# Where the scores of a pair's last 64 queries stand in an attention round (causal attention, then a PReLU MLP)

## The chip, the cores and the metric

The kernel runs on one core of a Trainium2 chip. The metric is the device time of one execution in microseconds (us). Before the change it is 618.56 us, the median of three runs (618.24 to 618.84). The profiled execution took 617.75 us; its span, from the first to the last instruction, is 616.0 us, so 1.75 us lie outside the span. Durations below come from that one execution.

## The reference

```python
scores = scale * np.matmul(q, k.transpose(0, 1, 3, 2))   # 4 batches, 12 heads, 448 queries, head size 64
scores = np.where(mask, -1000000000.0, scores)           # causal
attn = softmax(scores)                                   # max, exp, sum + 1e-9, division
x = np.matmul(attn, v) reshaped to (1792, 768)
h = x @ w_in                                             # w_in 768 x 2048
g = np.maximum(h, 0) + alpha * np.minimum(h, 0)
out = g @ w_out                                          # w_out 2048 x 768
```

All inputs are float64 in memory (the weights are taken apart into float32 parts on the chip) and the output is float32.

## The kernel before

**The two stages.** The attention takes the first 150 us of the span, the MLP the rest; some steps of the MLP's preparation are mixed into the attention: the weight pieces of `start_piece` go through ScalarE (Abs, line 250), GpSimd (clamp, line 253), four VectorE steps (lines 256, 260, 263 and 264) and a GpSimd addition (line 267).

**A pair.** The attention works on 24 pairs of heads. A pair has two heads j = 0, 1 and 448 queries in three blocks: 128 (i = 0), 128 (i = 1), 128 (i = 2), and a last block of 64 queries that both heads share (i = 3): their 64 queries each are laid side by side into one operand `qd` of 128 columns, loaded apart from the other queries (line 362). `scores(p, 0)` (S0) makes the scores of i = 1 and 0 for both heads and `scores(p, 1)` (S1) those of i = 2; both use 64 rows of the array per head (line 424), twelve matmul passes in all. `scores(p, 2)` (S2) makes the scores of the last queries, two passes of 128 rows (line 416). VectorE then masks and takes the maximum (MXij, line 436), ScalarE takes the exponential with its row sum (EXij, line 451), VectorE turns the sums into reciprocals (RC, lines 460 and 461), GpSimd multiplies (NOij, line 405), TensorE transposes (PTi, line 480, 16 passes), ScalarE and VectorE copy the transposes out of PSUM (Cij, lines 401 and 403: C10, C20 and C30 on ScalarE, C00 and C21 on VectorE), and TensorE multiplies with V (AV, line 499). XF, XN, XH and XL then write the result's parts for the MLP; XL (line 561) is the last reader of AV's bank.

**The round.** `attention()` runs rounds n = 0 to 27. The text `ORDER` lists the steps of a round by name with a lag: `S0+1` means S0 of pair n - 1. Each engine takes its instructions in the order of that text. `ROUNDS` has texts of their own for rounds 2 and 3, and round 26 is `ORDER` with one step moved. Before the change a round's order on each engine is, with the lag behind the plus sign:

- TensorE: AV+4, S2+2, PT1+3, PT0+3, PT2+3, PT3+3, S0+1, S1+1 (and SF+1, which is S2 for pairs 0 and 23 only)
- VectorE: MX11+2, MX20+2, MX21+2, MX00+2, MX01+2, XF or XN+4, MX30+2, EG, XL+4, C00+3, C21+3, RC+2, ED, MX10+1. EG and ED are the VectorE steps of the weight pieces; E2, at the head of the round, holds four of them in round 25
- ScalarE: EX10+2, EX11+2, EX20+2, EX00+2, EX21+2, EX01+2, XH+4, C10+3, EX30+2, C20+3, C30+3, EA
- GpSimd: NO00+3, NO10+3, NO21+3, NO11+3, NO20+3, NO30+3, weight work, NO01+2

Round 4 is the first with all steps; its AV is that of pair 0, at 16.08 us. Pair 23 has its S0, S1 and S2 in round 24.

**Banks.** Eight PSUM banks serve S (five per pair), PT (five) and AV (one). A bank goes to the next step in the program that asks for one, in about the order in which the last reader of each stands in the program, and the new owner's first matmul waits for that reader. S0 and S1 take two banks each, one per head.

**Loads.** SyncE issues the loads in program order: `LK` and `LQ` of pair n stand at the head of round n; `LQ` loads the two halves of `qr` and then the two pieces of `qd`.

Of the kernel before, what the change touches and what calls it, by code (L numbers as in the profile page):

```python
# [34 lines left out]
LOADV = {0: 3, 1: 2, 2: 2, 9: 4, 10: 3, 12: 2, 13: 3, 14: 2}  # L35
TURNS = [(0, 0), (0, 1), (0, 2), (0, 5), (1, 0), (1, 1), (1, 3), (1, 4), (0, 3), (0, 4), (1, 2), (1, 5)]
ORDER = """
E2+4 LK+0 LQ+0 LT+4 NO00+3p NO10+3p MX11+2 NO21+3p NO11+3p EX10+2 EX11+2 MX20+2 NO20+3p MX21+2 EX20+2 NO30+3p MX00+2 EX00+2 AV+4 S2+2 LV+4 PT1+3 PT0+3 PT2+3 EX21+2 MX01+2 EX01+2 XF+4 XN+4 XH+4 C10+3a MX30+2 EG+4 XL+4 EX30+2 EH+4 C00+3d C21+3d RC+2 ED+4 NO01+2p C20+3a PT3+3 S0+1 S1+1 SF+1 C30+3a EA+4 MX10+1 ST+4
"""
ROUNDS = {2: """  # L40
LK+0 LQ+0 MX11+2 EX10+2 EX11+2 MX00+2 EX00+2 MX01+2 EX01+2 MX20+2 EX20+2 MX21+2 EX21+2 RA+2 NO10+2p NO11+2p NO00+2p NO01+2p MX30+2 S0+1 S1+1 PT1+2 PT0+2 MX10+1 MX11+1 EX30+2 RB+2 NO20+2p NO21+2d NO30+2p
""", 3: """
LK+0 LQ+0 EX10+2 EX11+2 MX00+2 EX00+2 MX01+2 EX01+2 MX20+2 S2+2 EX20+2 MX21+2 PT2+3 EX21+2 C10+3a C00+3d MX30+2 EX30+2 C21+3d RC+2 NO01+2p C20+3a PT3+3 S0+1 S1+1 SF+1 C30+3a MX10+1
"""}
FIRST = """
0: gh.0Y gh.0X gl.0Y gl.0X abs.i0.1 clamp.i0.1 cast.o0.0 cast.o1.0 st
# [77 lines left out]
def kernel(  # L124
# [19 lines left out]
    NQ = S // QP  # L144
    LQ = S - NQ * QP
# [25 lines left out]
    def bank(name):  # L171
        return banks["a"].tile([P, 512], F32, tag="a", name=name)
# [176 lines left out]
    def half(j):  # L349
        return slice(j * D, (j + 1) * D)  # L350
# [59 lines left out]
    def scores(p, n):  # L410

        if n == 2:
            ps = bank(f"s_{p}_{n}")[:, :S]
            nc.tensor.matmul(ps, qd[p % 3], T["k", p], start=True, stop=True)  # L416
            T["s", p, NQ, 0] = ps
            return
        banks = [bank(f"s_{p}_{n}_{j}") for j in range(2)]
        o = 0  # L420
        for i in ((1, 0), (2,))[n]:
            lim = (i + 1) * QP
            for j, ps in enumerate(banks):
                nc.tensor.matmul(  # L424
                    ps[:, o : o + lim], T["q", p][half(j), i * QP : (i + 1) * QP],
                    T["k", p][half(j), :lim], start=(o == 0), stop=(n > 0 or i == 0),
                )
                T["s", p, i, j] = ps[:, o : o + lim]
            o += lim
# [26 lines left out]
    def row_rec(p, cols=slice(0, 2 * NQ + 1)):  # L456
        sm = T["sm", p]
        if ("r", p) not in T:
            T["r", p] = ap["b2"].tile([P, 2 * NQ + 1], F32, tag="rs", name=f"rs_{p}")
        nc.vector.tensor_tensor(out=sm[:, cols], in0=sm[:, cols], in1=least[:, cols], op=ALU.add)  # L460
        nc.vector.reciprocal(T["r", p][:, cols], sm[:, cols])
# [55 lines left out]
    def flush(to):  # L517
        while to:
            to.pop(0)()
# [62 lines left out]
    def run(it, n=None):  # L582
# [3 lines left out]
    steps = {  # L586
        "LV": load_v_next, "RC": row_rec, "RA": lambda p: row_rec(p, slice(0, 4)), "RB": lambda p: row_rec(p, slice(4, 2 * NQ + 1)), "AV": av, "XH": x_hi, "XN": x_hi_plain, "XF": x_sums, "XL": x_lo, "ST": lambda p: flush(stores),
    }
# [17 lines left out]
            add(steps, f"EX{i}{j}", row_exp, i, j)  # L606
            add(choice, f"NO{i}{j}", row_norm, i, j)
    edge = (0, len(pairs) - 1)
    steps["SF"] = lambda p: p in edge and scores(p, NQ - 1)
    steps["S2"] = lambda p: p in edge or scores(p, NQ - 1)  # L610
    steps["ED"] = lambda p: [fn() for fn in plan.pop(p + 4, ())]
    steps["EH"] = lambda p: [fn() for fn in mid.pop(p + 4, ())]
    steps["EG"] = lambda p: [fn() for fn in gap.pop(p + 4, ())]
# [4 lines left out]
    def order_of(text):  # L618
        order = []
        for w in text.split():  # L620
            name, lag = w.split("+")
            if name in choice:
                eng = {"a": nc.scalar, "d": nc.vector, "p": nc.gpsimd}[lag[-1]]
                order.append((int(lag[:-1]), name, lambda p, fn=choice[name], eng=eng: fn(p, eng)))
            else:
                order.append((int(lag), name, steps[name]))
        return order

    def attention(hooks):
        order, first = order_of(ORDER), {n: order_of(x) for n, x in ROUNDS.items()}  # L630
        first[26] = order_of(ORDER.replace("C10+3a ", "").replace("EH+4 ", "EH+4 C10+3a "))
        last = max(lag for lag, *_ in order)
        for n in range(len(pairs) + last):
            for lag, name, fn in first.get(n, order):
                if 0 <= n - lag < len(pairs):
                    fn(n - lag)
                    for hook in hooks.get((n - lag, name), ()):
                        hook()
# [282 lines left out]
    def after(p, name, fn, *args):  # L921
        hooks.setdefault((p, name), []).append(lambda: fn(*args))
# [4 lines left out]
    with tc.manual_schedule():  # L927
# [33 lines left out]
        last = len(pairs) - 1  # L961
# [5 lines left out]
        after(6, "LQ", load_next)  # L967
        after(3, "LV", lambda: nc.sync.dma_start(out=alpha_sb, in_=alpha.rearrange("(c p) -> p c", p=P)))
        after(20, "LV", lambda: ts(out=less, in0=alpha_sb[:, :GC], scalar1=-1.0, scalar2=None, op0=ALU.mult))
        after(last, "SF", scores_done)  # L970
        after(last - 1, "C30", h_plain, 0, 4)
        after(last - 1, "AV", h_plain, 4, 10)
        after(last, "C21", h_act, 0, "Y")
# [128 lines left out]
```

## Time and profile before

| What | Value |
|---|---|
| median of 3 runs | 618.56 us (618.24 to 618.84) |
| the profiled execution | 617.75 us, span 616.0 us |
| PE busy | 607.5 us (99%) |
| VectorE (DVE), ScalarE (ACT), GpSimd (POOL) busy | 498.5, 285.2, 391.2 us |
| granted TensorE clock, mean | 0.999 of full speed |
| chain that ended last | PE 91%, DVE 3%, DMA 2%, ACT 1%, issue 1%, POOL 1% |

PE is TensorE's matmuls, PEld its weight loads, SP is SyncE's queue. A matmul's end is modelled, so PE busy is no measure of its idle time inside a stage: the distance from one step's start to the next step's start is.

### The profile page before, as it was taken

To read this page: it belongs to the slowest core of one execution; us is meant where nothing else is said; L and a number is where in the kernel's file an instruction comes from. 1 tells how busy PE (TensorE), PEld (TensorE's weight loads), DVE (VectorE), ACT (ScalarE), POOL (GpSimd) and SP (SyncE) were. 2 spreads that over 40 slices of the span, in tenths; PEclk is the share of its full clock that TensorE was granted. 3 is DMA by queue.
4 is the path that set the end of the run, shared out by engine and by line. 5 is a ranking of instruction groups with operands and counts; after the bars stand their busy time and mean duration, and the time that the engine had idled before them with its cause. 6 is when DMAs were issued, how large, how long until landed. Compare 5 with 4: busy or idle time off the path is not lost.

```text
span 616.0 us, 10906 instructions
## 1 busy us (share of the span) xinstructions
PE 607.5 (99%) x3527; PEld 530.5 (86%) x3527; DVE 498.5 (81%) x1120; ACT 285.2 (46%) x782; POOL 391.2 (64%) x525
## 2 busy tenths in 40 slices
PE   8999999999999999999999999999999999999997
PEld 4666666667879999999999999999999999999997
DVE  5899999999777787898798789868987887895364
ACT  6989888896657643333232323232332323231110
POOL 6666587867475669756875686486668756862120
PEclk9999999999999999999999999999999999999999
DMA  7765477634884578657757756676576577554725
GB/s 171 197 191 164 131 216 215 191 123 130 271 294 153 182 248 276 197 170 226 216 160 231 224 167 204 209 229 198 171 228 217 156 231 225 165 174 140 245 89 193
DMA packets 88298, 120.40 MB, mean 195 GB/s; under 512 B 12273, under 2 KB 66257, under 8 KB 88241
## 3 DMA queue, kind: packets, MB, share of 16 engines
q1 hardware_dynamic: 87584, 118.36, 62.7%
q0 software_dynamic: 336, 0.89, 0.6%
q8 instruction: 28, 0.46, 0.3%
q10 hardware_dynamic: 320, 0.46, 0.2%
q14 instruction: 30, 0.24, 0.1%
HBM read 105.00 MB, written 14.68 MB: 194 GB/s over the span
## 4 chain that ended last, share of the span: by engine, by line
PE 91%; DVE 3%; DMA 2%; ACT 1%; issue 1%; POOL 1%; POOLq 0%; ACTq 0%; SPq 0%; DVEq 0%
PE o L789 35%; PE heldY L691 11%; PE heldX L691 8%; PE a L499 7%; PE pt L480 6%; PE heldZ L691 6%; PE s L424 5%; PE s L416 3%; PE h_V L691 3%; PE heldW L691 3%; PE h_Y L691 1%; PE h_W L691 1%; PE h_X L691 1%; PE h_Z L691 1%; DMA lo_T<-low_T 1%; ACT p L451 1%
## 5 line engine op out<-in xcount | busy, mean ns | idle before, releaser
L797 DVE TENSOR_TENSOR acc<-o,acc 128x384 f32<-128x384 f32 x196 | 107.4, 551 | 76.3 <-PE o L789 75.6
L405 POOL TENSOR_SCALAR p<-p,rs 128x128 f32<-128x128 f32 (+3 forms) x165 | 82.2, 520 | 42.2 <-ACT ptf L401 27.1
L451 ACT ACTIVATE p<-s,nm 128x256 f32<-128x256 f32 (+3 forms) x168 | 82.0, 497 | 14.8 <-DVE nm L436 13.2
L436 DVE CUSTOM_DVE_ANT_0 s<-s,mask 128x128 f32<-128x128 f32 (+3 forms) x168 | 71.2, 480 | 9.0 <-PE s L424 5.3
L789 PE MATMUL o<-wo,g_X 128*128 128x384 f32 x336 | 77.8, 339 | 0.5 <-DVE g_X L755 0.5
L789 PE MATMUL o<-wo,g_Z 128*128 128x384 f32 x336 | 77.5, 338 | 0.0
L789 PE MATMUL o<-wo,g_W 128*128 128x384 f32 x336 | 77.3, 337 | 0.3 <-POOL g_W L755 0.3
L789 PE MATMUL o<-wo,g_Y 128*128 128x384 f32 x336 | 76.9, 336 | 0.0
L789 PEld LDWEIGHTS o<-wo,g_X 128*128 128x128 f32 x336 | 60.7, 188 | 4.0 <-DVE g_X L755 0.8
L789 PEld LDWEIGHTS o<-wo,g_Z 128*128 128x128 f32 x336 | 60.7, 188 | 3.1
L789 PEld LDWEIGHTS o<-wo,g_W 128*128 128x128 f32 x336 | 60.6, 188 | 0.6 <-POOL g_W L755 0.6
L789 PEld LDWEIGHTS o<-wo,g_Y 128*128 128x128 f32 x336 | 60.6, 188 | 0.0
L480 PEld LDWEIGHTS pt<-ident,p 128*128 128x128 f32 x384 | 43.3, 140 | 12.5 <-issue 7.9
L499 PEld LDWEIGHTS a<-ptf,v 128*64 128x64 f32 x384 | 25.4, 136 | 31.0 <-issue 12.1
L267 POOL TENSOR_TENSOR y_i<-y_i,x_i 128x384 f32<-128x384 f32 x32 | 33.0, 1030 | 29.6 <-DVE x_i L264 29.6
L267 POOL TENSOR_TENSOR y_o<-y_o,x_o 128x384 f32<-128x384 f32 x32 | 33.4, 1042 | 25.4 <-DVE x_o L264 25.4
L480 PE MATMUL pt<-ident,p 128*128 128x128 f32 x384 | 47.3, 274 | 1.2 <-POOL p L405 0.8
L499 PE MATMUL a<-ptf,v 128*64 128x448 f32 (+3 forms) x384 | 46.8, 386 | 0.1
L424 PE MATMUL s<-kr,qr 64*128 64x384 f32 (+2 forms) x288 | 39.5, 395 | 0.7 <-DMA kr<-in_k_dram 0.5
L401 ACT ACTIVATE ptf<-pt 128x512 f32<-128x512 f32 (+1 forms) x72 | 38.1, 573 | 3.0 <-PE pt L480 2.9
L755 POOL TENSOR_TENSOR g_Z<-t_Z,g_Z 128x384 fp32r<-128x384 f32 (+1 forms) x15 | 18.5, 1231 | 31.4 <-ACT g_Z L750 31.4
L250 ACT ACTIVATE x_i<-raw_i 128x384 f32<-128x384 f32 x32 | 17.8, 556 | 42.6 <-DMA raw_i<-in_moe_w_in_dram 42.6
(189 smaller groups left out, 1340.2 us busy)
## 6 DMA issues: line engine op xcount, KB each, us to landing
lo_T<-low_T SPq DMA_DIRECT2D x28, 512.0 KB, 4.7
lo_B<-low_B SPq DMA_DIRECT2D x25, 512.0 KB, 5.0
raw_i<-in_moe_w_in_dram SPq DMA_DIRECT2D x32, 384.0 KB, 3.6
raw_o<-in_moe_w_out_dram SPq DMA_DIRECT2D x32, 384.0 KB, 3.6
lo_T<-low_T SPq DMA_DIRECT2D x28, 384.0 KB, 3.6
lo_B<-low_B SPq DMA_DIRECT2D x25, 384.0 KB, 4.0
lo_N<-low_N SPq DMA_DIRECT2D x16, 512.0 KB, 4.7
lo_N<-low_N SPq DMA_DIRECT2D x16, 384.0 KB, 4.5
```

The source lines that it names most:

```text
L267: nc.gpsimd.tensor_tensor(out=y, in0=y, in1=xf, op=ALU.add)
L401: eng.activation(out, x, AF.Copy, scale=side)
L405: eng.tensor_scalar(out=out, in0=x, scalar1=side, scalar2=1.0, op0=ALU.mult, op1=ALU.mult)
L424: nc.tensor.matmul(ps[:, o : o + lim], T["q", p][half(j), i * QP : (i + 1) * QP], T["k", p][half(j), :lim], start=(o == 0), stop=(n > 0 or ...
L436: nc.vector.tensor_tensor_reduce(out=t, in0=t, in1=masks[1] if i == NQ else masks[0][:, (NQ - 1 - i) * QP :], scale=-SCALE, scalar=MOST_F3 ...
L451: nc.scalar.activation(T["p", p, i][:, j, : t.shape[1]], t, AF.Exp, scale=-1.0, bias=T.pop(("nm", p, i, j)), accum_out=T["sm", p][:, z : z ...
L480: nc.tensor.transpose(ps[:, j - js[0], c], t[:, j, c * QP : (c + 1) * QP], T["ident"])
L499: nc.tensor.matmul(out[half(j), c * QP :], vs[b % 2][:, hp, c, j], x[:, c * QP : S], start=(c == 0), stop=(c == NQ),)
L691: nc.tensor.matmul(ps, w[:, u, k * P : (k + 1) * P], x, start=(first and i == 0), stop=(i == len(mms) - 1), skip_group_check=True,)
L755: eng.tensor_tensor(out=l, in0=hts.pop((q, nm)), in1=h, op=ALU.subtract)
L789: nc.tensor.matmul(ps[:, :NH], x, w, start=(i == 0), stop=(i == 3 * GC - 1))
L797: nc.vector.tensor_tensor(out=a[:, cols], in0=ps[:, :NH], in1=a[:, cols], op=ALU.add)
```

## The change

S2 moves from lag 2 to lag 1 and on TensorE to the place between PT3 and S0: AV+4, PT1+3, PT0+3, PT2+3, PT3+3, S2+1, S0+1, S1+1. MX30 moves from the middle of VectorE's round (lag 2, behind XF and XN) to its end, ahead of MX10 (lag 1). EX30 moves from behind C10 to the first place of ScalarE's round (lag 2). SF stays in round 1 only, for pair 0; pair 23 now has its S2 through the common step. Round 3 keeps the old place for pair 1 (as SG) and has the new one for pair 2, so round 3 has two S2, where before round 24 had two. The hook `scores_done` (it closes the pools of the attention's inputs) hangs on the last S1 in place of the last SF. The count of instructions is the same.

```diff
-... NO21+3p NO11+3p EX10+2 EX11+2 ... EX00+2 AV+4 S2+2 LV+4 PT1+3 ... C10+3a MX30+2 EG+4 XL+4 EX30+2 EH+4 ... PT3+3 S0+1 S1+1 SF+1 C30+3a EA+4 MX10+1 ST+4
+... NO21+3p NO11+3p EX30+2 EX10+2 EX11+2 ... EX00+2 AV+4 LV+4 PT1+3 ... C10+3a EG+4 XL+4 EH+4 ... PT3+3 S2+1 S0+1 S1+1 C30+3a EA+4 MX30+1 MX10+1 ST+4
-ROUNDS = {2: """
+ROUNDS = {1: """
+LK+0 LQ+0 S0+1 S1+1 SF+1 MX10+1
+""", 2: """
...
-... MX20+2 S2+2 EX20+2 ... PT3+3 S0+1 S1+1 SF+1 C30+3a MX10+1
+... MX20+2 SG+2 EX20+2 ... PT3+3 S2+1 S0+1 S1+1 C30+3a MX30+1 MX10+1
...
-    steps["SF"] = lambda p: p in edge and scores(p, NQ - 1)
-    steps["S2"] = lambda p: p in edge or scores(p, NQ - 1)
+    steps["SF"] = lambda p: p == 0 and scores(p, NQ - 1)
+    steps["SG"] = steps["S2"] = lambda p: scores(p, NQ - 1)
...
-        after(last, "SF", scores_done)
+        after(last, "S1", scores_done)
```

## Rows read from the trace of the kernel before

**Rows 1.** Busy time of the engines in a stretch: stretch, length, engines, clock, DMA.
```profile
46.00:58.00 12.00, 12.00 (x94) 8.09 (x92) 11.64 (x45) 11.25 (x39) 7.27 (x15) 1.00 0.54 164
```
**Rows 2.** The chain that ended last, attention: start, length, what.
```profile
76.91 1.88 PE a L499 x16
78.79 0.95 PE s L416 x2
79.74 1.75 PE pt L480 x16
81.49 1.50 PE s L424 x12
...
101.22 1.88 PE a L499 x16
...
107.65 1.88 PE a L499 x16
...
120.00 1.88 PE a L499 x16
```
**Rows 3.** ScalarE and VectorE in one steady round, in order of time.
```profile
77.25 0.47 ACT L451 ACTIVATE p<-s,nm 128x256 f32<-128x256 f32 x1 [0.67 <-DVE nm L436]
79.78 0.63 DVE L436 CUSTOM_DVE_ANT_0 s<-s,mask 128x448 f32<-128x448 f32 x1 [0.25 <-PE s L416]
80.77 0.63 ACT L451 ACTIVATE p<-s,nm 128x448 f32<-128x448 f32 x1
81.92 0.20 DVE L461 RECIPROCAL rs<-sm 128x7 f32<-128x7 f32 x1
```
**Rows 4.** GpSimd's seven normalizations of two rounds, in order of time.
```profile
76.51 3.47 POOL L405 TENSOR_SCALAR p<-p,rs 128x128 f32<-128x128 f32 x7 [2.87 <-DVE rs L461]
...
108.05 3.38 POOL L405 TENSOR_SCALAR p<-p,rs 128x128 f32<-128x128 f32 x7 [2.12 <-DVE rs L461]
```
**Rows 5.** Passes of S2 (30 to 136 us): shortest, median, longest ns.
```profile
L416 PE MATMUL s<-kr,qd x36: 539/591/643, 30.1 to 134.4; 128*128 128x448 f32 x36
```
**Rows 6.** Passes of the transposes: a steady round, then round 25, which has no S2.
```profile
L480 PE MATMUL pt<-ident,p x16: 272/272/273, 79.6 to 81.2; 128*128 128x128 f32 x16
L480 PE MATMUL pt<-ident,p x6: 272/272/328, 147.1 to 147.7; 128*128 128x128 f32 x6
```
**Rows 7.** TensorE at the end of round 3, in order of time.
```profile
13.57 0.70 PE L424 MATMUL s<-kr,qr 64*128 64x256 f32 x2
14.45 1.53 PE L424 MATMUL s<-kr,qr 64*128 64x256 f32 x10 [0.19 <-DMA qr<-in_q_dram]
16.08 0.60 PE L499 MATMUL a<-ptf,v 128*64 128x448 f32 x2
```
**Rows 8.** The last qd piece of pair 2: its issue, and us to its landing.
```profile
9.09 0.60 SPq L362 DMA_DIRECT2D qd<-in_q_dram  x1
qd<-in_q_dram SPq DMA_DIRECT2D x1, 16.0 KB, 5.9
```
**Rows 9.** The qd loads issued from 20 to 137 us.
```profile
DMA to landing us min/median/max: 1.9/2.2/4.1
```
**Rows 10.** TensorE in round 24 and behind it, in order of time.
```profile
144.23 1.02 PE L416 MATMUL s<-kr,qd 128*128 128x448 f32 x2
145.18 1.95 PE L499 MATMUL a<-ptf,v 128*64 128x448 f32 x16
```
**Rows 11.** The chain that ended last, end of the attention.
```profile
147.41 0.68 ACT p L451 x2
...
148.22 0.95 PE pt L480 x6
...
149.28 0.63 PE pt L480 x4
149.90 1.05 PE h_Y L691 x6
```
**Rows 12.** The third VectorE step of the weight pieces (30 to 145 us).
```profile
L263 DVE TENSOR_SCALAR x_i<-y_i x4: 354/356/1511, 37.8 to 104.6; 128x384 int32<-128x384 int32 x4
```

More of the change, by code (lines that the diff above doesn't have):

```diff
@@ L37 @@
 ORDER = """
-E2+4 LK+0 LQ+0 LT+4 NO00+3p NO10+3p MX11+2 NO21+3p NO11+3p EX10+2 EX11+2 MX20+2 NO20+3p MX21+2 EX20+2 NO30+3p MX00+2 EX00+2 AV+4 S2+2 LV+4 PT1+3 PT0+3 PT2+3 EX21+2 MX01+2 EX01+2 XF+4 XN+4 XH+4 C10+3a MX30+2 EG+4 XL+4 EX30+2 EH+4 C00+3d C21+3d RC+2 ED+4 NO01+2p C20+3a PT3+3 S0+1 S1+1 SF+1 C30+3a EA+4 MX10+1 ST+4
+E2+4 LK+0 LQ+0 LT+4 NO00+3p NO10+3p MX11+2 NO21+3p NO11+3p EX30+2 EX10+2 EX11+2 MX20+2 NO20+3p MX21+2 EX20+2 NO30+3p MX00+2 EX00+2 AV+4 LV+4 PT1+3 PT0+3 PT2+3 EX21+2 MX01+2 EX01+2 XF+4 XN+4 XH+4 C10+3a EG+4 XL+4 EH+4 C00+3d C21+3d RC+2 ED+4 NO01+2p C20+3a PT3+3 S2+1 S0+1 S1+1 C30+3a EA+4 MX30+1 MX10+1 ST+4
 """
-ROUNDS = {2: """
+ROUNDS = {1: """
+LK+0 LQ+0 S0+1 S1+1 SF+1 MX10+1
+""", 2: """
 LK+0 LQ+0 MX11+2 EX10+2 EX11+2 MX00+2 EX00+2 MX01+2 EX01+2 MX20+2 EX20+2 MX21+2 EX21+2 RA+2 NO10+2p NO11+2p NO00+2p NO01+2p MX30+2 S0+1 S1+1 PT1+2 PT0+2 MX10+1 MX11+1 EX30+2 RB+2 NO20+2p NO21+2d NO30+2p
 """, 3: """
-LK+0 LQ+0 EX10+2 EX11+2 MX00+2 EX00+2 MX01+2 EX01+2 MX20+2 S2+2 EX20+2 MX21+2 PT2+3 EX21+2 C10+3a C00+3d MX30+2 EX30+2 C21+3d RC+2 NO01+2p C20+3a PT3+3 S0+1 S1+1 SF+1 C30+3a MX10+1
+LK+0 LQ+0 EX10+2 EX11+2 MX00+2 EX00+2 MX01+2 EX01+2 MX20+2 SG+2 EX20+2 MX21+2 PT2+3 EX21+2 C10+3a C00+3d MX30+2 EX30+2 C21+3d RC+2 NO01+2p C20+3a PT3+3 S2+1 S0+1 S1+1 C30+3a MX30+1 MX10+1
 """}
```

## The prediction, as it was made before the result

> **What bounds the kernel now.** I read the chain of waits first, since the work is moved and not made less. From 16 us on it runs on TensorE from round to round, and a round of the attention is four pieces: AV 1.88, S2 0.95, the transposes 1.75, S0 and S1 1.50, in sum 6.08 us [rows 2]. Then the busy time by stretches: in two such rounds TensorE has no gap, VectorE is busy 11.64 of 12.00 us and ScalarE 11.25 [rows 1]. So TensorE sets the round, with two engines close behind it. The time lines of the engines show where these two wait: VectorE 0.25 us for S2 ahead of MX30, ScalarE 0.67 us for the first maximum of the round [rows 3]. In a round that TensorE fills, a wait of theirs costs nothing, and taking it away brings nothing. What can change is (a) the length of the four pieces in another order, (b) the head, where TensorE still waits for loads, (c) the few rounds that are longer than 6.08, (d) the end of the attention.
>
> **(a) The order on TensorE: -1.0 us.** The instructions are the same, so only what stands exposed between pieces can differ. S2 behind AV: one pass of its two takes 643 ns and the other 539 [rows 5], so about 0.104 us of its weight load lies open. The transposes behind S2 are all 272 or 273 ns: nothing is open. Round 25 has no S2, and there the first transpose behind AV takes 328 where the rest take 272: 0.056 us open [rows 6]. In the new order it is the transposes that follow AV in every round, and S2 follows transposes of the same 128 rows, where its load can go ahead under them as theirs now goes under S2. That saves 0.104 - 0.056 = 0.048 us in each of 21 rounds (4 to 24), 1.0 us. Bounds: S2 could keep its open load (0.056 more per round, 1.2 us lost), or the transposes' load could vanish too (0.104, 2.2 us gained). The trace has no S2 in front of S0 in a full round; I take that change of shape at what the one from the transposes to S0 costs, so at nothing. I take 0.048, since both its parts are rows of the same pieces.
>
> By the Trainium skill's page "TensorE: Matmul & The Clock Gate", section "LDWEIGHTS (loading the stationary operand)", the load's time hangs on the number of columns alone, 128 / 1.2 = 107 ns here. The 0.104 us of S2 agrees with it, the 0.056 us of the transposes does not. By the page the exchange would save nothing; the trace's own pair is nearer to this kernel, and I follow that.
>
> **(b) The head: +1.4 us.** Round 3 now ends with PT3(0), S0(2), S1(2). S0 starts at 13.57, its second head waits for the load of qr until 14.45, and AV(0) starts at 16.08 [rows 7]. After the change S2(2) stands in front of S0(2), and it needs both pieces of qd, the last of which is issued at 9.09 and lands 5.9 us later, at about 15.0 [rows 8]. TensorE takes its matmuls in order, so S0 and S1 wait behind it: 15.0 + 0.95 + 1.50 = 17.45 to 17.5 in place of 16.08 [rows 2]. Nothing hides this: it is the one place where the extra S2 isn't in a filled round. Bounds: had qd landed by 13.57, S2 would cover most of the hole ahead of 14.45, and some 0.2 us would be left (0.95 less the wait of 14.45 - 13.57, of which S0's first head uses a part); with the hole and the landing 0.3 later, 1.7. From round 4 on, qd lands 1.9 to 4.1 us after its issue [rows 9], and its issue stands nearly a round ahead of S2, so no later S2 waits for a load.
>
> **(c) The longer rounds: -0.54 us.** AV to AV is 107.65 - 101.22 = 6.43 in one round, 0.35 too long; the two rounds to 120.00 take 12.35, 0.19 too long [rows 2]. The first has the one VectorE step of 1511 ns, where 354 is usual [rows 12]; XL came late behind it, and a score matmul needs XL's bank. With MX30 (0.63 us and its wait, [rows 3]) no longer between XN and XL, XL comes some 0.8 us earlier in the round while S1's place in the round hardly moves, so 0.35 is covered. Bounds: 0 to -0.54; I take all of it.
>
> **The moved steps in a full round: 0.** S2 ends 1.5 us ahead of the round's end, MX30 takes 0.63 there in VectorE's former wait, and EX30 takes 0.63 where ScalarE now waits 0.67 [rows 3]. No engine gets more work. Their waits in the new order: MX10 behind MX30, for which EX10 and all later exponentials wait. S2 ends about half a microsecond ahead of S0's first block, so MX10 moves little. The transposes lose S2 as cover: they start 0.95 earlier behind AV and need GpSimd's NO10 and NO11. GpSimd's seven start 0.40 ahead of AV and end 3.07 behind its start [rows 2, 4]; the last of them is for PT3, which comes 1.88 + 0.75 x 1.75 = 3.19 behind it: just in time even if GpSimd stays where it is. But it starts on the reciprocals, which now come at 81.92 behind EX30 (80.77, 0.63 long) and the copies of the transposes; both move ahead by 0.9 or more [rows 3]. Banks: the transposes then take over from EX30, EX20 and EX00, and S2 from EX21, which all stand earlier than their takers by a microsecond or so. If this cover is gone, the cost is that of rival 1 below.
>
> **(d) The end: -0.4 us beyond the shift.** At round 24's S0 the sum so far is -1.0 + 1.4 - 0.54 = about -0.1. Round 24 then lacks its second S2 of 0.95 (from 144.23 to 145.18, [rows 10]), but the last pair's exponentials are late: the transposes stop at 148.22 for ScalarE and once more at 149.28, and the MLP's first matmul comes at 149.90 [rows 11]. These waits go back to MX10 of the last pair and four VectorE steps behind it, which keep their distance from S0. So the 0.95 isn't won. What is won is one place in the handing on of banks: EX30, already done, frees the first, and the event that let the last transposes go at 149.28 now lets the MLP's first matmul go, whose place was 149.90. That would be 0.6; I take 0.4, as the maxima stand a little later behind MX30. Bounds 0 and -0.6.
>
> **The sum.** -1.0 + 1.4 - 0.54 - 0.4 = -0.5 us. From there TensorE is filled through the MLP and the shift stays. The profiled execution (span 616.0 and 1.75 around it, 617.75) would take 617.2; the median of the runs shown is 0.8 above it, so 618.56 - 0.5 = 618.0.
>
> **The rivals.**
> 1. No saving between the pieces, or the transposes wait for GpSimd by a like amount: for it, that GpSimd is late at 108.05, 0.40 behind its AV at 107.65 [rows 2, 4]; against it, that this was the round of the long hole. 618.0 + 1.0 = 619.0. The page's rule on weight loads gives the same time.
> 2. Faster: the transposes' open load hides as well, 0.104 x 21 = 2.2 instead of 1.0, or the head costs 0.2 and not 1.4. For it: the load of a transpose is short, and landings at the head depend on how the transfers fall. Against: round 25 shows the 0.056 plainly. 618.0 - 1.2 = 616.8.
> 3. Slower: VectorE becomes the bound. Its free time is 0.18 us a round [rows 1], and a weight step took 1511 ns once instead of 356 [rows 12], at a cost of 0.35 us to TensorE [rows 2]. GpSimd's work moves by 0.9 us against VectorE's, and if its additions now fall on these steps in most of the rounds that have one (about eight), 8 x 0.35 = 2.8 us are lost: 618.0 + 2.8 = 620.8. It decides from five such steps on. Against it: one in four was hit before, and XL now has 0.8 us more room.
>
> **The chances.** Forecast 0.44, rival 1 0.18, rival 2 0.22, rival 3 0.16. A measurement of this kernel can tell 0.2% from no change, 1.24 us. Rival 2 lies beyond it on one side, with 0.03 of the forecast's own spread: faster 0.25. Rival 3 lies beyond on the other: slower 0.16. The rest, 0.59, is within. The range takes in the forecast and rivals 1 and 2 with a little more at each end, 616.5 to 619.9, and leaves out most of rival 3.
>
> **What would show it.** AV to AV of 6.03 in place of 6.08 in full rounds shows (a), and 6.08 refutes it. AV(0) at 17.5 with TensorE waiting for qd shows (b); AV(0) near 16.3 refutes it. No round of 6.4 shows (c). The MLP's first matmul at about 149.4, with the waits of the last transposes at ScalarE, shows (d). Rounds above 6.08 with VectorE named as the releaser, and many weight steps above 1 us, would make the prediction wrong on the slow side; TensorE waiting for GpSimd at the first transposes would show rival 1.

## The result, and the profile after

The changed kernel takes 625.54 us, the median of five runs (624.83 to 627.33). The kernel before took 618.56 beside it (five runs, 617.66 to 618.84). The ratio is 1.0123, interval 1.0109 to 1.0136: slower by 1.2%, outside the forecast range. The profiled execution took 627.33 us, span 625.5, and is the longest of its five; against the 616.0 us span of before, 9.5 us have to be found. The distances between TensorE's steps divide them:

| us | before | after | difference |
|---|---|---|---|
| AV(0) starts | 16.08 | 19.20 | +3.12 |
| AV(0) to AV(20), 20 rounds | 122.08 | 127.44 | +5.36 |
| AV(20) to AV(21) | 7.02 | 6.42 | -0.60 |
| AV(21) to the MLP's first matmul | 4.48 | 5.93 | +1.45 |
| from there to the first output matmul | 35.32 | 35.58 | +0.26 |
| from there to the end | 431.00 | 430.96 | -0.04 |

So the loss lies in the attention, most of it in its rounds. First the chain of waits there (start, length, what), against [rows 2]:

```profile
25.86 1.88 PE a L501 x16
27.74 1.90 PE pt L482 x16
...
30.39 1.50 PE s L426 x12
31.89 1.88 PE a L501 x16
...
56.39 1.88 PE a L501 x16
58.27 2.15 PE pt L482 x16
...
61.18 1.64 PE s L426 x10
62.82 1.88 PE a L501 x16
```

Two kinds of round are seen. From 25.86 to 31.89 a round takes 6.03 us, as step (a) said. From 56.39 to 62.82 it takes 6.43: the transposes and the scores are drawn out. Of the twenty rounds from AV(0) on, six take 6.03, twelve take 6.35 to 6.86, one 6.21, and the first 6.60 (the clock, below). The rounds differ in the weight work, in how many sums XF makes, and in one thing more: in two of three pairs (16 of 24) the result's high part is written by ScalarE (XH); in the others VectorE writes it itself (XN).

The passes of TensorE, against [rows 5] and [rows 6] (shortest, median, longest ns):

```profile
L418 PE MATMUL s<-kr,qd x36: 539/540/643, 29.5 to 138.1; 128*128 128x448 f32 x36
L482 PE MATMUL pt<-ident,p x16: 272/273/330, 58.2 to 60.2; 128*128 128x128 f32 x16
```

S2's median pass falls from 591 to 540, and one transpose shows 330: TensorE does what was forecast. But the busy time by stretches (stretch, length, engines, clock, DMA), against [rows 1], shows the others with less work done in the same 12 us:

```profile
46.00:58.00 12.00, 12.00 (x90) 7.76 (x90) 10.59 (x40) 9.99 (x36) 6.67 (x14) 1.00 0.52 161
```

VectorE is down from 11.64 to 10.59 of 12.00. It isn't short of work, so it waits. Its waits from 25 to 150 us (in total, times, longest) name one place:

```profile
DVE low_B L563 <- ACT xw L403: 7.8, 9, 1.3
DVE low_B L563 <- ACT wi_x L403: 2.8, 4, 0.8
```

This is XL waiting for XH, 10.6 us in 13 rounds. Before, the same two lines have one wait of 0.5 us; VectorE's waits there were 2.9 us for S2, spread over ten rounds. The time line of VectorE in one such round, from MX30 to the next MX30:

```profile
56.03 0.60 DVE L438 CUSTOM_DVE_ANT_0 s<-s,mask 128x448 f32<-128x448 f32 x1
...
58.85 1.15 DVE L555 TENSOR_TENSOR acc<-a,acc 128x448 f32<-128x448 f32 x2
60.74 0.62 DVE L563 TENSOR_TENSOR low_B<-a,xw 128x448 fp32r<-128x448 f32 x1 [0.75 <-ACT xw L403]
61.29 0.88 DVE L405 COPY ptf<-pt 128x256 f32<-128x256 f32 x2
...
62.46 0.61 DVE L438 CUSTOM_DVE_ANT_0 s<-s,mask 128x448 f32<-128x448 f32 x1
```

and ScalarE beside it:

```profile
56.81 0.64 ACT L453 ACTIVATE p<-s,nm 128x448 f32<-128x448 f32 x1 [0.72 <-DVE nm L438]
...
59.79 0.40 ACT L453 ACTIVATE p<-s,nm 128x128 f32<-128x128 f32 x1
60.13 0.58 ACT L403 ACTIVATE xw<-a 128x448 fp32r<-128x448 f32 x1
```

VectorE comes round in 62.46 - 56.03 = 6.43, the length of TensorE's round; it has no other gap. It ends XF (L555) at 60.00, and XL can't start before XH (60.13, 0.58 long) has made the high part. Now the kernel before, in the like round (VectorE, then ScalarE):

```profile
54.53 1.16 DVE L553 TENSOR_TENSOR acc<-a,acc 128x448 f32<-128x448 f32 x2
55.61 0.62 DVE L436 CUSTOM_DVE_ANT_0 s<-s,mask 128x448 f32<-128x448 f32 x1
56.15 0.14 DVE L436 DVE_READ_ACCUMULATOR2_ANT nm<- 128x1 f32 x1
56.36 0.62 DVE L561 TENSOR_TENSOR low_B<-a,xw 128x448 fp32r<-128x448 f32 x1
```
```profile
55.78 0.54 ACT L401 ACTIVATE xw<-a 128x448 fp32r<-128x448 f32 x1 [0.20 <-DVE acc L553]
```

MX30 stands exactly beside XH: 55.61 to 56.3 against 55.78 to 56.32, and XL follows without a wait. MX30 was the work that VectorE did while ScalarE wrote the high part. The change took it out, and 0.75 us of nothing stands in its place. [rows 3] are from a round without XH; there is no such gap to be seen in them.

A wait at XL and a long round don't go together one for one. The 6.03 us round from 25.86 has an XH too, and XL waits 0.99 us in it: VectorE's own round, from one reciprocal (RC) to the next, is 6.40 there, and 5.18 behind it, where the pairs have no XH and VectorE catches up. Where XH stands in several rounds on end (from 43.89, 94.97 and 121.16) the first takes 6.03 or 6.21 and those behind it are long. Three long rounds have no XH: 6.55 from 82.39, 6.75 from 107.64 and 6.77 from 114.38. In the VectorE round from 107.23, ahead of the last of them, VectorE is busy for 7.21 of 7.23 us, with a long weight step in it (shown below).

XH has its own reason to be late. It waits for XF in the row above, though it uses nothing that XF makes: both read AV's bank. The Trainium skill's page "PSUM — Partial Sum Buffer", section "PSUM bank collisions raise a hardware error", says that two engines may not touch one bank and quadrant at once, reads against reads included, and that the compiler's scheduler therefore makes the one depend on the other. The row agrees: two readers, and the second starts 0.09 us after the first ends.

The head, against [rows 7] and [rows 8]: TensorE in order of time, then the issue of pair 2's qd pieces with the time to their landing:

```profile
15.71 0.99 PE L418 MATMUL s<-kr,qd 128*128 128x448 f32 x2 [1.75 <-DMA qd<-in_q_dram]
16.63 2.64 PE L426 MATMUL s<-kr,qr 64*128 64x256 f32 x12
19.20 1.53 PE L501 MATMUL a<-ptf,v 128*64 128x448 f32 x3
```
```profile
L364 SPq DMA_DIRECT2D qd<-in_q_dram x2: 547/572/596, 8.3 to 8.9; - x2
...
DMA to landing us min/median/max: 6.7/6.9/7.0
```

S2 stands 1.75 us for qd, as forecast, and then S0 and S1 take 2.57 in place of 1.50. The granted clock is why; the same view by stretches:

```profile
12.00:16.00 4.00, 2.25 (x14) 1.54 (x14) 3.27 (x15) 3.75 (x15) 1.14 (x2) 1.00 1.19 186
16.00:20.00 4.00, 4.00 (x17) 1.69 (x17) 2.27 (x9) 2.14 (x8) 3.37 (x7) 0.62 0.88 188
```

Of the 9.5 us, the 1.07 that S0 and S1 lose here and 0.57 in the round behind come with this fall of the clock; the execution at the median had a mean clock of 1.000.

The end of the attention on TensorE, against [rows 10] and [rows 11]:

```profile
153.06 1.95 PE L501 MATMUL a<-ptf,v 128*64 128x448 f32 x16
...
155.85 0.66 PE L482 MATMUL pt<-ident,p 128*128 128x128 f32 x4 [0.47 <-POOL p L407]
156.71 0.55 PE L482 MATMUL pt<-ident,p 128*128 128x128 f32 x3 [0.20 <-POOL p L407]
157.87 1.27 PE L482 MATMUL pt<-ident,p 128*128 128x128 f32 x7 [0.61 <-ACT p L453]
158.99 0.97 PE L693 MATMUL h_Y<-xw,wi_A 128*128 128x384 f32 x4
```

and the third weight step, against [rows 12]: it still has one long instance, at 111.1, among the long rounds.

```profile
L265 DVE TENSOR_SCALAR x_i<-y_i x4: 347/526/1812, 40.5 to 111.1; 128x384 int32<-128x384 int32 x4
```

### The profile page after: what moved, and what is told of

Read it like the earlier page. It is cut to its first block, busy times and chain, and to the rows that moved or that the text cites. A ratio compares the mean times of both kernels' runs of the same rounds, so it can differ in the third digit from the quotient of the medians.

```text
span 625.5 us, 10888 instructions
## 1 busy us (share of the span) xinstructions
PE 614.7 (98%) x3527; PEld 531.3 (85%) x3527; DVE 500.1 (80%) x1120; ACT 282.4 (45%) x782; POOL 390.1 (62%) x525
## 4 chain that ended last, share of the span: by engine, by line
PE 93%; DVE 3%; DMA 1%; POOL 1%; issue 1%; ACT 1%; POOLq 0%; SPq 0%; DVEq 0%; ACTq 0%
PE o L791 36%; PE heldY L693 11%; PE heldX L693 8%; PE pt L482 7%; PE a L501 6%; PE s L426 6%; PE heldZ L693 5%; PE heldW L693 3%; PE h_V L693 3%; PE s L418 2%; PE h_Y L693 1%; PE h_W L693 1%; PE h_X L693 1%; PE h_Z L693 1%; DMA qd<-in_q_dram 1%
## 5 line engine op out<-in xcount | busy, mean ns | idle before, releaser
L453 ACT ACTIVATE p<-s,nm 128x128 f32<-128x128 f32 (+3 forms) x168 | 81.2, 503 | 28.1 <-DVE nm L438 27.7
L438 DVE CUSTOM_DVE_ANT_0 s<-s,mask 128x256 f32<-128x256 f32 (+3 forms) x168 | 70.1, 483 | 7.3 <-PE s L426 6.1
L482 PE MATMUL pt<-ident,p 128*128 128x128 f32 x384 | 52.5, 281 | 2.5 <-POOL p L407 1.7
L482 PEld LDWEIGHTS pt<-ident,p 128*128 128x128 f32 x384 | 41.0, 140 | 10.9 <-POOL p L407 5.3
L426 PE MATMUL s<-kr,qr 64*128 64x128 f32 (+2 forms) x288 | 42.1, 410 | 0.0
L426 PEld LDWEIGHTS s<-kr,qr 64*128 64x128 f32 x288 | 26.1, 195 | 16.5 <-ACT ptf L403 6.5
```

The costliest lines, as they stand in the source:

```text
L426: nc.tensor.matmul(ps[:, o : o + lim], T["q", p][half(j), i * QP : (i + 1) * QP], T["k", p][half(j), :lim], start=(o == 0), stop=(n > 0 or ...
L438: nc.vector.tensor_tensor_reduce(out=t, in0=t, in1=masks[1] if i == NQ else masks[0][:, (NQ - 1 - i) * QP :], scale=-SCALE, scalar=MOST_F3 ...
L453: nc.scalar.activation(T["p", p, i][:, j, : t.shape[1]], t, AF.Exp, scale=-1.0, bias=T.pop(("nm", p, i, j)), accum_out=T["sm", p][:, z : z ...
L482: nc.tensor.transpose(ps[:, j - js[0], c], t[:, j, c * QP : (c + 1) * QP], T["ident"])
```

## The experiments

Three theories stood at the start. The ring theory (the expectations call it the loop theory): MX30 now leads ScalarE's seven exponentials, XH comes after all of them, and XL, RC and the next MX30 after XH; that ring is 6.43 us long, so XH has to stand earlier. The cover theory: the transposes have lost S2 ahead of them and wait for GpSimd. The head theory: the late AV(0) is most of the loss. The gap theory came out of the first four experiments and was put to the next four: whatever XH waits for, VectorE has nothing to do between XF and XL since MX30 left; other work between the two is enough. The distances of all runs (us, one profiled execution each; a ratio is to the kernel before as run beside that kernel, whose median was 618.35 beside the first four experiments, 618.47 beside the next four and 617.78 beside the last three):

```
                  time (median)   AV(0)  20 rounds  20->21  21->MLP  MLP->out   ratio to before [interval]
before               618.56       16.08   122.08     7.02     4.48     35.32
after                625.54       19.20   127.44     6.42     5.93     35.58    1.0123 [1.0109, 1.0136]
xh_early             627.18       17.76   127.84     6.56     5.84     35.37    1.0134 [1.0113, 1.0155]
s2_alone             619.78       17.85   122.20     6.10     5.72     35.33    1.0016 [1.0006, 1.0025]
mx_ex_alone          625.84       18.00   127.59     6.41     5.92     35.34    1.0114 [1.0099, 1.0129]
head_s2_last         626.14       17.76   128.53     6.42     5.91     35.51    1.0120 [1.0100, 1.0140]
xl_late              619.46       17.78   121.25     6.03     5.01     36.36    1.0015 [1.0006, 1.0024]
xl_mid               621.95       17.85   122.92     6.09     5.71     36.68    1.0055 [1.0038, 1.0072]
before_uncovered     627.89       16.58   131.21     7.02     4.76     35.34    1.0149 [1.0134, 1.0164]
xl_late_r4           618.58       16.31   121.43     6.03     5.02     36.23    1.0001 [0.9992, 1.0011]
xl_late_r4_e2        621.11       16.48   121.43     6.03     3.60     40.89    1.0049 [1.0037, 1.0062]
before_e2            619.47       16.41   122.74     7.03     3.60     37.14    1.0025 [1.0015, 1.0034]
after_e2             626.97       17.89   126.35     6.42     3.87     40.04    1.0142 [1.0127, 1.0157]
```

**XH earlier (xh_early).** The changed kernel with XH ahead of two exponentials:

```diff
-... PT2+3 EX21+2 MX01+2 EX01+2 XF+4 XN+4 XH+4 C10+3a ...
+... PT2+3 XH+4 EX21+2 MX01+2 EX01+2 XF+4 XN+4 C10+3a ...
```

> The changed kernel with one step moved: XH, ScalarE's rounding copy of the attention result, stands ahead of EX21 instead of behind EX01; everything else is as changed. Loop theory: the long rounds (6.42 us) are a ring of waits between VectorE and ScalarE: MX30, EX30 and six more exponentials, XH, XL, C00, C21, RC, MX30. With XH ahead of EX21 the ring is cut, XL no longer waits 0.75 us, and rounds with XH come back to 6.03; their excess between AV(0) and AV(20) sums to about 6 us, so 625.5 - 5.6 = 619.9 (619 to 621). Cover theory (the transposes lost S2 as cover and wait for GpSimd): the order on TensorE is the same, so 625.5 as now (624.5 to 626.5). Head theory (the late start of AV(0) is most of it): 625.5 too.

627.18 us (625.89 and 626.42 in the two of its four executions with a mean clock of 1.000), and the ring theory's remedy fails. The time lines of VectorE and ScalarE show why:

```profile
58.12 1.16 DVE L555 TENSOR_TENSOR acc<-a,acc 128x448 f32<-128x448 f32 x2 [0.84 <-ACT xw L403]
59.19 0.61 DVE L563 TENSOR_TENSOR low_B<-a,xw 128x448 fp32r<-128x448 f32 x1
```
```profile
57.52 0.56 ACT L403 ACTIVATE xw<-a 128x448 fp32r<-128x448 f32 x1
```

XL no longer waits, but XF now does, 0.84 us, for XH: the two readers of AV's bank have changed places in the program and so in time. VectorE's gap has moved from behind XF to ahead of it. This is also the other direction of the order seen in the kernel before.

**Half of the change at a time (s2_alone, mx_ex_alone).** The first moves S2 on TensorE only, and leaves MX30 and EX30 where they were; the second moves MX30 and EX30 and leaves S2 behind AV (of the pair whose S0 and S1 follow in the same round, since MX30 now comes that early):

```diff
-... EX30+2 EX10+2 ... XH+4 C10+3a EG+4 XL+4 EH+4 ... S2+1 S0+1 S1+1 ... MX30+1 MX10+1 ST+4
+s2_alone:    ... EX10+2 ... XH+4 C10+3a MX30+2 EG+4 XL+4 EX30+2 EH+4 ... S2+1 S0+1 S1+1 ... MX10+1 ST+4
+mx_ex_alone: ... EX30+2 EX10+2 ... AV+4 S2+1 LV+4 ... EG+4 XL+4 EH+4 ... S0+1 S1+1 ... MX30+1 MX10+1 ST+4
```

> Half of the change: S2 stands between the transposes and S0 of its pair's round on TensorE, but MX30 and EX30 stay where they were before (behind XF and XN, and behind XL). Loop theory: MX30 and EX30 are off the ring, rounds are 6.03 and the time is that of before plus the head (1 to 2 us) less the shorter rounds (1 us): 618.5 to 620.5. Cover theory: the transposes have lost S2 as cover as in the changed kernel, so rounds of 6.4 stay: 624 to 626.

> The other half: MX30 and EX30 stand as changed (end of VectorE's round, first of ScalarE's), S2 of the next pair stands behind AV and ahead of the transposes, so that the transposes have it as cover again. Loop theory: the ring is whole, rounds with XH stay at 6.4: 624 to 626. Cover theory: rounds go back to 6.08: 619 to 620.5.

S2's move alone keeps the rounds (122.20, most of them 6.03 to 6.12) and costs 0.16%; in its profile AV(0) is 1.77 us late, and the end takes 0.32 more. MX30's and EX30's move alone has the whole loss of the rounds (127.59), with 10.8 us of XL's waits, although S2 covers the transposes again. So the loss of the rounds isn't TensorE's order, and the cover theory falls.

**S2 behind S1 in round 3 (head_s2_last).**

```diff
-... PT3+3 S2+1 S0+1 S1+1 C30+3a MX30+1 MX10+1
+... PT3+3 S0+1 S1+1 S2+1 C30+3a MX30+1 MX10+1
```

> The changed kernel with the order of round 3 alone altered: S2 of pair 2 behind its S0 and S1, not ahead of them. Head theory: TensorE no longer waits for qd with S0 and S1 behind it, AV(0) comes at about 17.0 us (19.2 in the profile of the changed kernel, whose clock had fallen there), and the time falls by 0.5 to 2 us from 625.5: 623.5 to 625.0. Loop theory says the same for the head and that no more than this is won: the later rounds stay at 6.4. If the head is most of the loss: 619.

A miss: AV(0) comes at 17.76, as in the other runs with S2 ahead of S0. S0 then waits for its own load, and S2's 0.95 still stands ahead of AV(0). The first two rounds behind it were 6.82 and 6.71 us, with waits of 1.26 and 1.42 us at XL in them; why these are longer than in the changed kernel (0.61 and 0.99) is not settled.

**XL behind VectorE's copies (xl_late, xl_mid).** The test of the gap theory: 0.8 us of copies, C00 and C21, stand between XF and XL; nothing of ScalarE's order is touched. In xl_mid one of the two:

```diff
-... XH+4 C10+3a EG+4 XL+4 EH+4 C00+3d C21+3d RC+2 ...
+xl_late: ... XH+4 C10+3a EG+4 EH+4 C00+3d C21+3d XL+4 RC+2 ...
+xl_mid:  ... XH+4 C10+3a EG+4 EH+4 C00+3d XL+4 C21+3d RC+2 ...
```

> The changed kernel with XL (VectorE's rounding remainder of the attention result) behind C00 and C21 instead of ahead of them. Gap theory: VectorE's instructions fill 5.7 of a round's 6.03 us; in rounds with XH it stands still 0.75 us ahead of XL, because XH on ScalarE starts only when XF on VectorE has ended, and MX30, which before filled that gap, is gone. 5.7 + 0.75 = 6.42. With the two copies in the gap the rounds come back to 6.03: 5 to 6 us less than 625.5, 619 to 621. Cover theory (the transposes lost S2 and wait for GpSimd): nothing changes, 625.5. Theory that ScalarE's longer head of the round (EX30 first) is the bound: nothing changes either, 625.5.

> The changed kernel with XL between C00 and C21: one copy of 0.44 us stands in the gap of 0.75. Gap theory: rounds with XH take 6.42 - 0.40 = 6.03 to 6.1, so the time is within 1 us of that with both copies in the gap: 619.5 to 621.5. The other theories: 625.5.

xl_late came out as the gap theory said: with the whole gap covered the rounds are 6.03, all but one of 6.65, and the time is 619.46. xl_mid went the way it said and not as far: with half of the gap covered XL's waits are still 5.9 us, four rounds take 6.34 to 6.97, and the time, 621.95, lies outside the expected range. EX30 still stands first on ScalarE and S2 ahead of S0 in xl_late, so neither place by itself makes the rounds long. VectorE in the stretch of [rows 1], xl_late:

```profile
46.00:58.00 12.00, 12.00 (x93) 7.94 (x92) 11.82 (x46) 11.40 (x39) 7.28 (x16) 1.00 0.55 161
```

**The gap opened in the kernel before (before_uncovered).** MX30 behind XL instead of ahead of it, nothing else:

```diff
-... XH+4 C10+3a MX30+2 EG+4 XL+4 EX30+2 ...
+... XH+4 C10+3a EG+4 XL+4 MX30+2 EX30+2 ...
```

> The kernel before with one step moved: MX30 behind XL instead of ahead of it. S2, EX30 and all else as before. Gap theory: the gap ahead of XL opens in this kernel too; VectorE needs 5.7 + 0.6 to 0.75 in rounds with XH, 6.3 to 6.4 in place of 6.08, in some 13 rounds: 621.5 to 623.5. Cover theory and the theory of ScalarE's head: S2 still covers the transposes and EX30 isn't first, so 618.5.

The gap is there again, with S2 where it always was:

```profile
59.48 0.62 DVE L561 TENSOR_TENSOR low_B<-a,xw 128x448 fp32r<-128x448 f32 x1 [0.67 <-ACT xw L401]
60.03 0.62 DVE L436 CUSTOM_DVE_ANT_0 s<-s,mask 128x448 f32<-128x448 f32 x1
```

The size is more than expected, 9.4 us for 4 or so. MX30 is late by the gap as well, and EX30, which stands ahead of C20 and C30 on ScalarE, with it; AV then waits for a copy:

```profile
55.66 1.95 PE L499 MATMUL a<-ptf,v 128*64 128x448 f32 x16 [0.50 <-ACT ptf L401]
```

From 25 to 150 us such waits (in total, times, longest) are:

```profile
PE a L499 <- ACT ptf L401: 6.2, 14, 0.5
```

That is the gap and this second wait together; the runs don't part the two.

**Both remedies (xl_late_r4).** xl_late, and pair 2 keeps its S2 behind AV in round 4, so that round 4 and not round 3 has two:

```diff
-3: ... PT3+3 S2+1 S0+1 S1+1 C30+3a MX30+1 MX10+1
+3: ... PT3+3 S0+1 S1+1 C30+3a MX10+1
+4: ... EX10+2 ... AV+4 SG+2 ... C10+3a MX30+2 EG+4 XL+4 EX30+2 ... S2+1 S0+1 S1+1 ... MX30+1 MX10+1 ST+4
```

> As the one with XL behind C00 and C21, and pair 2 keeps its S2, MX30 and EX30 at the old place (round 4); pair 3 is the first at the new place, so that the round with two S2 is round 4 and not round 3. Head theory: AV(0) comes at 16.1 again, the extra S2 of 0.95 us stands in round 4: 0.7 us less than with pair 2 moved, so 618.5 to 620. If the head does not matter: the same as there.

AV(0) stands at 16.31, round 4 takes 6.83, and the next rounds take 6.03. In VectorE's time line the copies fill the gap, and XL has no wait:

```profile
55.30 1.16 DVE L557 TENSOR_TENSOR acc<-a,acc 128x448 f32<-128x448 f32 x2
56.37 0.93 DVE L407 COPY ptf<-pt 128x256 f32<-128x256 f32 x2
57.22 0.61 DVE L565 TENSOR_TENSOR low_B<-a,xw 128x448 fp32r<-128x448 f32 x1
```

618.58 us, a ratio of 1.0001: the loss is gone, and there is no gain. The MLP's first matmul comes 0.87 us earlier than before (148.79), but the next stretch is 0.91 longer.

**The end (xl_late_r4_e2, before_e2, after_e2).** In round 25 four VectorE steps of a weight piece (E2) stand between the last pair's first maximum and its others. They go behind RC:

```diff
+first[25] = order_of(ORDER.replace("E2+4 ", "").replace("RC+2 ", "RC+2 E2+4 "))
```

> xl_late_r4 with one more edit: in round 25 the four VectorE steps of the weight piece (2.35 us, 143.57 to 145.92 in xl_late_r4) stand behind RC and no longer ahead of the last pair's five maxima. If these steps are what holds the end up, the last pair's exponentials come up to 2.35 us earlier, TensorE no longer waits 0.62 for ScalarE at the last transposes, and AV(21) to the MLP's first matmul takes 3.7 to 4.1 us instead of 5.02: 0.9 to 1.3 us off, about 617.5 us, 0.1 to 0.25% under the kernel before. Rival: GpSimd's normalizations or the copies of the transposes hold the bank instead; then 4.7 to 5.0 and 618.3 to 618.7 us.

> The kernel before with the same edit alone (the control: does the edit pay without the change?). AV(21) to the MLP's first matmul 4.48 in the kernel before, of which 0.63 is MX30 and EX30 of the last pair and 0.8 waits; by the theory 3.6 to 4.0, 617.9 us. Rival: no change, 618.3 to 618.7 us.

> The changed kernel with the same edit alone: it tells where the 1.45 us went that its end is longer (5.93 against 4.48 us). If the four steps hold up the maxima there too, the end falls to 4.3 to 4.9 us (TensorE's two waits for GpSimd, 0.47 and 0.20, may stay) and the time to 624.3 to 624.8 us. If the end waits for GpSimd's normalizations (reciprocals late behind XL), it stays at 5.4 to 5.9 and 625.2 to 625.6 us.

The place was right and the gain a miss. In all three the end shrinks, to 3.60, 3.60 and 3.87 us; in xl_late_r4_e2 TensorE runs through:

```profile
143.94 1.95 PE L503 MATMUL a<-ptf,v 128*64 128x448 f32 x16
145.82 1.97 PE L484 MATMUL pt<-ident,p 128*128 128x128 f32 x16
147.54 0.94 PE L696 MATMUL h_Y<-xw,wi_A 128*128 128x384 f32 x4
```

But the stretch behind it grows by 4.7, 1.8 and 4.5 us, more than was won (1.4, 0.9 and 2.1). Waits of TensorE from 147 to 200 us in xl_late_r4_e2:

```profile
PE pt L484 <- DVE ptf L407: 2.1, 1, 2.1
PE h_W L696 <- DMA lo_B<-low_B: 1.0, 1, 1.0
```

In xl_late_r4_e2 TensorE thus waits for VectorE's copy for the last transposes, and in all three the MLP reaches the low parts before they have come back from memory: it waits 1.0 us for them here, 1.5 in before_e2 and 3.0 in after_e2. The edit is the four steps alone; by which path they make the low parts late is not followed here. In the two kernels that grow by 4.7 and 4.5 the granted clock fell behind these waits as well, to 0.50 from 166 to 169 us and from 171 to 173.5; in before_e2, which grows by 1.8, it stayed at 1.00. Of the six executions of xl_late_r4_e2, the two with a mean clock of 1.000 took 619.60 and 619.99 us, the four with 0.996 or 0.997 took 620.98 to 621.99. The time at the end was not free to take.

## Why the prediction was wrong, step by step

**The step that failed: "The moved steps in a full round: 0."** It took MX30's old place on VectorE for a wait for S2 with a mask step behind it, and asked only what the engines would do at the new places. What MX30 did at its old place for its neighbours was not asked. Work that stands between two steps that must keep a distance is cover, and taking it away costs the distance: 0.75 us in the round shown, 10.6 us in 13 rounds with XH, of which 5.36 us came through to TensorE's twenty rounds (0.57 of that is the clock). It was readable beforehand: ScalarE's `xw` row and VectorE's MX30 row of before, side by side. The round that I read [rows 3] was one without XH, and I took it for all. mx_ex_alone, xl_late and before_uncovered show the step's failure from three sides: the loss comes with MX30's move, goes when other work covers XH, and comes without the change when the cover is taken away.

What holds XH up in the changed kernel differs from round to round. In the round shown, two paths end together: XF at 60.00, whose bank XH reads, and the last exponential, behind which XH stands without idle time at 60.13. In another round it is ScalarE alone:

```profile
71.63 0.62 DVE L555 TENSOR_TENSOR acc<-a,acc 128x448 f32<-128x448 f32 x1
72.92 0.57 ACT L403 ACTIVATE xw<-a 128x448 fp32r<-128x448 f32 x1
```

XF ends at 72.25, XH starts 0.67 us later, directly behind an exponential, and XL waits 1.27 us. XH starts 0.57 to 0.67 behind XF's end at 79.78, 98.16 and 105.03 as well. So the ring theory had a part of the wait in these rounds; xh_early says only that moving XH alone doesn't help.

**(a) right.** -0.048 a round was forecast; the full rounds are 6.03 against 6.08, in every kernel whose VectorE keeps up. mx_ex_alone, with S2 back behind AV, has 6.08 as its shortest round, so it is S2's place that makes the difference. The sentence on the Trainium skill's "TensorE: Matmul & The Clock Gate", section "LDWEIGHTS (loading the stationary operand)", would have had 6.08 stay; the measurement decides for the rows of the pieces.

**(b) right in its place, short in its size.** +1.4 forecast for AV(0); the six profiles with this head and an undisturbed clock have 17.76 to 18.00, +1.7 to +1.9, at or just above the upper bound of 1.7 that was given. The last piece of qd lands at 15.25 to 15.49 in them instead of 15.0, and S2 starts 0.08 to 0.09 behind its landing in each. The profiled execution of the changed kernel is 1.4 later than xl_late's: its last piece landed at 15.62, 6.7 us after its issue instead of 5.9, so S2 starts 0.35 later than in xl_late (15.71 against 15.36), and S0 and S1 take 2.64 for 1.57 at the fallen clock, which also adds 0.57 to the first round.

**(c) wrong in the changed kernel.** The long rounds were to vanish as XL came 0.8 earlier. XL came later, and 6.64 to 6.77 stand in their place. Under xl_late_r4, whose longest weight step of this kind took 1126 ns, no round after round 4 is above 6.03; xl_late, with one of 1815 ns, has a round of 6.65. That a round with a step of 1511 ns would have been covered is not shown.

**(d) wrong in the changed kernel, right in its size without the gap.** From AV(20) to the MLP: 11.50 before, 12.35 after; 11.04 in xl_late and 11.05 in xl_late_r4, which is the -0.4 forecast. In both, the last transposes stop once for ScalarE, 0.62 us, and not twice. s2_alone, with MX30, EX30 and XL at their old places, has 11.82; that fits a gain by EX30's early place, as the step said, but no run parts EX30 from XL. What the step and the sum left out is behind it: the shift was to stay through the MLP, and its first stretch took 0.9 to 1.0 us more in both xl_late kernels. Of that, 0.76 and 0.63 us are waits of TensorE for the copies of the last pair's transposes (0.20 for ScalarE's, 0.56 and 0.43 for VectorE's), which the kernel before doesn't have.

**The rivals.** Rival 1's wait of the transposes for GpSimd is seen once in the twenty rounds, 0.40 us at 117.10. Rival 3 had the right engine as the bound, and the right sign, with the wrong mechanism: it priced VectorE by collisions of its weight steps with GpSimd (2.8 us in all), not by a wait of VectorE itself. The number that mattered stood in it, VectorE's 0.18 us of free time a round: a new gap of 0.75 can't be taken up by that, and 0.35 to 0.40 of it shows in the round (6.43 against 6.08 and 6.03). The sum with the gap closed, xl_late: 1.70 - 0.83 - 0.46 + 1.04 - 0.24 = +1.21 us of span, against -0.5 forecast. With the head mended too: -0.1.

## What to carry to other kernels

Before moving a step, ask what it covers: look at both neighbours on its engine, and at whatever another engine does beside it that the later neighbour needs. Look at one round of every kind, not at one steady round, as steps that run in two pairs of three are not in all of them. Where an engine off the path has 0.2 us to spare in a round, its order has to be checked as TensorE's is.

## What the runs showed of the hardware that I had not expected

The granted clock of TensorE fell to 0.50, the lower of its two levels (1.2 in place of 2.4 GHz), from 17 to 20 us, behind 1.75 us without work out of the four before (12 to 16); from 16 to 20 its mean is 0.62. xl_late has the same order there and a wait of 1.52 us, and its clock stayed at 1.00. (Its row names ScalarE for the wait; the last piece of qd lands at 15.27, 0.09 ahead of S2, as in the other runs.)

```profile
15.36 0.99 PE L418 MATMUL s<-kr,qd 128*128 128x448 f32 x2 [1.52 <-ACT p L453]
16.28 1.57 PE L426 MATMUL s<-kr,qr 64*128 64x256 f32 x12
17.78 1.95 PE L501 MATMUL a<-ptf,v 128*64 128x448 f32 x16
```

The length of the wait alone doesn't decide it: mx_ex_alone waits 1.83 us at the same place and xl_mid 1.97, and both keep a clock of 1.00 from 12 to 20 us; behind waits of 2.13 and 2.96 us in xl_late_r4_e2 and after_e2 it fell, behind 1.55 in before_e2 it did not. What decides is not shown. So a wait of 2 us or less cost about its length again in the profiled execution (1.07 us in S0 and S1 and 0.57 in the round behind) and only itself in others. Of the changed kernel's five executions three have a mean clock of 1.000, one 0.999, and only the profiled one 0.996.
